# Finishing the last three output tiles of an attention kernel by column parts

## The chip, the cores and the metric

The kernel runs on one core of a Trainium2 chip. The metric is the device time of one execution in microseconds (us); the profile's span, from the first to the last instruction, is some 1.8 us shorter. Times of one kernel lie up to 1.3 us from their median (the kernel before), which matters here. So beside the time I use one stretch of each trace that does not contain the 915 us before it: from the first matmul of tile B, the first tile that the change touches, to the end of the span. Spans are given to 0.1 us, so differences of the stretch below that mean nothing.

## The reference, cut to what matters

```
xn = layernorm(x)                               # x: 2048 x 640
s  = attention(xn @ wq, k_cache, v_cache) @ wo  # 32 heads of 192, the last 512 keys
g  = silu(swiglu_ffn(xn))
return x + s * g                                # 2048 x 640, bf16
```

The output has 16 tiles of 128 rows by 640 columns. At the end of the kernel the product with `wo` for the last head pairs is still to come, and after it, tile by tile, the multiply by g and the add of a sum, `sacc`, that already holds x and the other heads' part times g.

## The kernel before: the end

```
def sc_tile():                       # two PSUM buffers of this kind, each of two halves
    return psum.tile([P, 2, 512], f32, name="sc", tag="sc")
def mm_tile():                       # and two of this kind
    return psum.tile([P, 2, 512], f32, name="mm", tag="mm")
...
def wo_mm(ps, i, qt, n, first=True, end=True):      # HD = 320 columns
    for j in range(3):
        nc.tensor.matmul(ps, OTs[i][:, 3 * qt + j, :],
            pairs[i // NB]["wo"][:, j, n * HD : (n + 1) * HD], start=..., stop=...)
...
def wo_last(b, qt, eng):
    ...
    split = b == NB - 1 and qt == 3                 # the very last tile
    sc = None if split else sc_tile()
    ps = [(mm_tile()[:, 0, :] if split else sc[:, n, :])[:, 0:HD] for n in range(2)]
    for n, cols in enumerate(halves):
        if late(i):
            wo_mm(ps[n], i - NB, qt, n, end=False)
        wo_mm(ps[n], i, qt, n, first=not late(i))
        if split:
            nc.vector.tensor_tensor(s_f[:, n, :], ps[n], g2[:, t, cols], ALU.mult)
            nc.vector.tensor_tensor(ob[:, cols], s_f[:, n, :], sacc[:, t, cols], ALU.add)
            (nc.scalar if n else nc.sync).dma_start(out=..., in_=ob[:, cols])
    if split:
        return
    nc.vector.tensor_tensor(s_f[:], sc[:, :, 0:HD], g2[:, t, :]..., ALU.mult)
    eng.tensor_tensor(ob[:], s_f[:]..., sacc[:, t, :], ALU.add)
    stores.append((t, ob))
...
for b in (2, 3):
    for qt in range(4):
        store(0 if (b, qt) == (3, 3) else 3)
        wo_last(b, qt, V if b == 3 and qt % 2 == 0 else G)   # V: VectorE, G: GpSimd
```

The last four tiles, (b, qt) = (3, 0) to (3, 3), are called A, B, C and D. Before the change A, B and C are done whole, and only D by halves. D's halves: each calls `mm_tile()` for itself, so each has a PSUM tile of its own.

The softmax here doesn't subtract the row's maximum and nothing guards it: scores larger than these inputs give would overflow.

Of the kernel before, what the change touches and what calls it, by code (L numbers as in the profile page):

```python
# [10 lines left out]
ALU = mybir.AluOpType  # L11
# [4 lines left out]
def kernel(  # L16
# [13 lines left out]
    nc = tc.nc  # L30
    P = nc.NUM_PARTITIONS

    x2 = A_x.flatten_outer_dims()
    out2 = out.flatten_outer_dims()
    Sq, D = x2.shape
# [9 lines left out]
    NB = Sq // 512  # L45
# [5 lines left out]
    HD = D // 2  # L51
    scale = float(Dh) ** -0.5
    EPS = 1e-5
    bf = dt.bfloat16
    f32 = dt.float32
# [6 lines left out]
    kk, vv, wq, wo = A_k_cache[0], A_v_cache[0], A_wq, A_wo  # L62
# [8 lines left out]
    def sc_tile():  # L71
        return psum.tile([P, 2, 512], f32, name="sc", tag="sc")

    def mm_tile():
        return psum.tile([P, 2, 512], f32, name="mm", tag="mm")
# [5 lines left out]
    g2 = res.tile([P, T, D], bf, name="g2")  # L81
# [14 lines left out]
    pairs = {}  # L96
# [68 lines left out]
    with ExitStack() as fctx:  # L165
# [154 lines left out]
        first = {f: [sc[:, s, :] for s in range(2)] for f, sc in ((0, sc_tile()), (1, sc_tile()))}  # L320
# [89 lines left out]
    finp = ctx.enter_context(tc.tile_pool(name="fin", bufs=2))  # L410
    sacc = sapool.tile([P, T, D], f32, name="sacc")

    NS = NPAIR * NB
    turn_t = smpool.tile([P, 1], f32, name="turn_t", bufs=1)
    last = NPAIR - 1
    Ps, OTs, Obs, xrs = {}, {}, {}, {}
# [89 lines left out]
    def pv_full(i, q2):  # L506

        pr, b = divmod(i, NB)
        if q2 == 0:
            Obs[i] = opool.tile([P, 4, 2, Dh], bf, name="O_b")  # L510
            tag = "OT_l" if late(i) and pr < last else "OT_b"
            OTs[i] = otpool.tile([P, 12, P], bf, name=tag, tag=tag, bufs=2 if tag == "OT_l" else 3)
        O_b, OT_b = Obs[i], OTs[i]
        alone = i < 2 or (pr == last and 2 * b + q2 < 5)
        acc = sc_tile() if alone and q2 and b < 2 else mm_tile()
        for k in range(2):
            qt = 2 * q2 + k
            for h in range(2):
                for kc in range(KC):
                    nc.tensor.matmul(  # L520
                        acc[:, k, h * 256 : h * 256 + Dh + 1],
                        Ps[i][kc][:, h, qt * P : (qt + 1) * P], V_p[:, kc, h, 0 : Dh + 1],
                        start=(kc == 0), stop=(kc == KC - 1),
                    )
        divide(i, q2, acc, alone)
# [6 lines left out]
    def late(i):  # L532
        return i // NB >= NPAIR - 2 and i % NB >= 2

    def wo_mm(ps, i, qt, n, first=True, end=True):
        for j in range(3):
            nc.tensor.matmul(  # L537
                ps, OTs[i][:, 3 * qt + j, :], pairs[i // NB]["wo"][:, j, n * HD : (n + 1) * HD],
                start=(first and j == 0), stop=(end and j == 2),
            )  # L540

# [54 lines left out]
    def wo_full(i, qt):  # L596
        pr, b = divmod(i, NB)
        t = 4 * b + qt
        sc = sc_tile()
        for n in range(2):  # L600
            wo_mm(sc[:, n, 0:HD], i, qt, n)
        s_t = sacc[:, t, :].rearrange("p (n d) -> p n d", n=2)
        if pr == 0:
            nc.vector.tensor_copy(out=s_t, in_=sc[:, :, 0:HD])
        else:
            nc.vector.tensor_tensor(s_t, s_t, sc[:, :, 0:HD], ALU.add)

        if pr == last - 1 or late(i + NB):
            nc.gpsimd.tensor_tensor(sacc[:, t, :], sacc[:, t, :], g2[:, t, :], ALU.mult)
            if pr < last - 1:  # L610
                add_x(t)
# [6 lines left out]
    def wo_last(b, qt, eng):  # L618
        i, t = last * NB + b, 4 * b + qt
        ob = xrs[t] if b < 2 else finp.tile([P, D], bf, name="ob", bufs=4)  # L620
        s_f = finp.tile([P, 2, HD], f32, name="s_f", bufs=4)
        halves = [slice(n * HD, (n + 1) * HD) for n in range(2)]
        split = b == NB - 1 and qt == 3
        sc = None if split else sc_tile()
        ps = [(mm_tile()[:, 0, :] if split else sc[:, n, :])[:, 0:HD] for n in range(2)]
        for n, cols in enumerate(halves):
            if late(i):
                wo_mm(ps[n], i - NB, qt, n, end=False)
            wo_mm(ps[n], i, qt, n, first=not late(i))
            if split:  # L630
                nc.vector.tensor_tensor(s_f[:, n, :], ps[n], g2[:, t, cols], ALU.mult)
                nc.vector.tensor_tensor(ob[:, cols], s_f[:, n, :], sacc[:, t, cols], ALU.add)
                (nc.scalar if n else nc.sync).dma_start(
                    out=out2[t * P : (t + 1) * P, cols], in_=ob[:, cols]
                )
        if split:
            return
        nc.vector.tensor_tensor(  # L638
            s_f[:], sc[:, :, 0:HD], g2[:, t, :].rearrange("p (n d) -> p n d", n=2), ALU.mult
        )  # L640
        eng.tensor_tensor(ob[:], s_f[:].rearrange("p n d -> p (n d)"), sacc[:, t, :], ALU.add)
        stores.append((t, ob))

    def store(left):
        while len(stores) > left:
            t, ob = stores.pop(0)
            nc.sync.dma_start(out=out2[t * P : (t + 1) * P, :], in_=ob[:])
# [19 lines left out]
    for pr in range(NPAIR):  # L667
        for b in range(NB):
            i = pr * NB + b
# [23 lines left out]
        for b in range(NB):  # L693
            i = pr * NB + b
# [15 lines left out]
    i = last * NB  # L710
    V, G = nc.vector, nc.gpsimd
# [3 lines left out]
    for b, q2, more in ((0, 0, (2, 1)), (0, 1, (3, 0)), (1, 0, (3, 1)), (1, 1, None)):  # L715
        for k in range(2):
            wo_last(b, 2 * q2 + k, G)
        if more:
            pv_full(i + more[0], more[1])
    for b in (2, 3):  # L720
        for qt in range(4):
            store(0 if (b, qt) == (3, 3) else 3)
            wo_last(b, qt, V if b == 3 and qt % 2 == 0 else G)


# [28 lines left out]
```

## Time and profile before

| | before |
|---|---|
| time, median of the 5 runs beside the changed kernel | 927.31 us (926.93 to 928.28) |
| span in the trace | 925.4 us |
| from tile B's first matmul (915.53) to the end | 9.87 us |
| last store issued at | 922.63 us |
| from that issue to the end of the span | 2.77 us |

In the timeline a row gives the start, the duration (of a merged group, from its first start to its last end), engine, line, what is written and read, the shape, and in brackets the idle time of the engine before the row and what ended it. In the chain of waits a row is start, length, and the work that the end depended on; "issue" is the short time between a release and the start.

### The profile page before, as it was taken

How to read it: one execution, taken by the hardware profiler on the slowest of the kernel's cores; microseconds unless marked ns; L12 is line 12 of the kernel's file. 1: busy time of each engine (PE TensorE's matmuls, PEld its weight loads, DVE VectorE, ACT ScalarE, POOL GpSimd, SP SyncE). 2: the span in 40 equal slices, each digit the busy share in tenths (PEclk: the TensorE clock that was granted, in tenths of full speed). 3: DMA queues.
4: the chain of work that ended last, by engine and by line, in shares of the span. 5: the costliest groups of instructions: out<-in, count | busy, mean ns of one | idle time of the engine just before them, and what ended most of it. 6: DMA issues, size and time to landing. Idle time of an engine off the chain costs nothing.

```text
span 925.4 us, 25770 instructions
## 1 busy us (share of the span) xinstructions
PE 917.3 (99%) x11085; PEld 624.9 (68%) x11101; DVE 575.6 (62%) x844; ACT 473.8 (51%) x847; POOL 100.1 (11%) x387
## 2 busy tenths in 40 slices
PE   9999999999999999999999999999999999999997
PEld 5455556575858585868686867676767777776665
DVE  6433331467676767676766667676767676767655
ACT  4222222556464646565555565656555555556561
POOL 0000000000000000000000000000000000002976
PEclk9999999999999999999999999999999999999999
DMA  9321510044544445444536262536362717162624
GB/s 298 72 56 33 114 35 1 1 77 89 87 79 83 83 80 86 75 90 70 95 60 106 59 107 55 111 53 113 46 119 42 124 36 129 36 129 76 135 57 140
DMA packets 243810, 77.18 MB, mean 83 GB/s; under 512 B 224624, under 2 KB 243696, under 8 KB 243696
## 3 DMA queue, kind: packets, MB, share of 16 engines
q1 hardware_dynamic: 242640, 74.72, 41.5%
q8 instruction: 87, 1.43, 0.7%
q10 hardware_dynamic: 1056, 0.82, 0.3%
q14 instruction: 27, 0.22, 0.1%
HBM read 39.45 MB, written 2.62 MB: 45 GB/s over the span
## 4 chain that ended last, share of the span: by engine, by line
PE 98%; DMA 1%; DVE 0%; issue 0%; ACT 0%; DVEq 0%
PE mm L428 22%; PE sc L563 19%; PE sc L442 18%; PE mm L468 16%; PE sc L276 11%; PE mm L298 6%; PE sc L537 3%; PE mm L520 2%; DMA wg_sb<-in_B_w_gate_dram 1%; PE mm L276 0%; PE mm L311 0%; DMA OT_b<-O_b 0%; PE sc L520 0%; DMA x_t<-in_A_x_dram 0%; DVE s_f L638 0%
## 5 line engine op out<-in xcount | busy, mean ns | idle before, releaser
L446 ACT ACTIVATE p_t<-sc 128x1024 bf16<-128x1024 f32 x254 | 253.0, 1022 | 130.5 <-PE sc L442 130.5
L433 DVE TENSOR_REDUCE qT<-mm 128x512 bf16<-128x1024 f32 x189 | 231.2, 1223 | 104.8 <-PE mm L428 102.4
L498 ACT ACTIVATE O_b<-mm,r 128x192 bf16<-128x192 f32 x486 | 164.6, 421 | 183.1 <-issue 159.9
L428 PE MATMUL mm<-xnT,wq_p 64*128 64x512 bf16 x1890 | 237.7, 377 | 0.0
L563 PE MATMUL sc<-wo_p,OT_b 64*128 64x320 bf16 x2592 | 217.4, 296 | 0.5 <-DMA OT_b<-O_b 0.5
L588 DVE TENSOR_TENSOR sacc<-sacc,sc 128x640 f32<-128x640 f32 x200 | 164.1, 821 | 78.3 <-PE sc L563 78.3
L442 PE MATMUL sc<-qT,khat 64*128 64x512 bf16 x1524 | 198.3, 377 | 0.0
L468 PE MATMUL mm<-V_p,p_t 64*128 64x193 bf16 x3520 | 186.4, 243 | 0.0
L468 PEld LDWEIGHTS <-p_t 64*128 64x128 bf16 x3584 | 162.6, 94 | 12.0
L428 PEld LDWEIGHTS <-wq_p 64*128 64x128 bf16 x1890 | 105.6, 94 | 96.0 <-issue 0.5
L563 PEld LDWEIGHTS <-OT_b 64*128 64x128 bf16 x2592 | 139.9, 94 | 22.7 <-DMA OT_b<-O_b 1.1
L442 PEld LDWEIGHTS <-khat 64*128 64x128 bf16 x1536 | 85.6, 94 | 79.2 <-issue 2.9
L551 POOL MEMSET turn_t<- 128x1 f32 x328 | 32.2, 98 | 697.9 <-PE mm L468 474.6
L284 DVE TENSOR_TENSOR hT<-sc,sg 128x512 bf16<-128x512 f32 x46 | 31.7, 690 | 85.2 <-ACT sg L283 85.1
L283 ACT ACTIVATE sg<-sc 128x512 bf16<-128x512 f32 x46 | 27.3, 596 | 72.4 <-PE sc L276 72.4
L276 PE MATMUL sc<-xnT,wg_sb 128*128 128x512 bf16 (+1 forms) x248 | 58.6, 354 | 1.0 <-DMA wg_sb<-in_B_w_gate_dram 0.4
L276 PE MATMUL sc<-xnT,wu_sb 128*128 128x512 bf16 (+1 forms) x259 | 59.1, 355 | 0.1
L298 PE MATMUL mm<-wd_sb,hT 128*128 128x320 bf16 x384 | 56.6, 300 | 0.0
L487 DVE RECIPROCAL r<-mm 128x4 f32<-128x4 f32 x124 | 22.7, 183 | 48.1 <-PE mm L468 36.3
L298 PEld LDWEIGHTS <-hT 128*128 128x128 bf16 x384 | 37.5, 98 | 18.9
L276 PEld LDWEIGHTS <-wu_sb 128*128 128x128 bf16 x285 | 26.3, 98 | 26.9
L276 PEld LDWEIGHTS <-wg_sb 128*128 128x128 bf16 x285 | 26.3, 98 | 23.5 <-DMA wg_sb<-in_B_w_gate_dram 0.5
(67 smaller groups left out, 373.1 us busy)
## 6 DMA issues: line engine op xcount, KB each, us to landing
wo_p<-in_A_wo_dram SPq DMA_DIRECT2D x16, 480.0 KB, 4.6
K_p<-in_A_k_cache_dram SPq DMA_DIRECT2D x32, 192.0 KB, 3.4
V_p<-in_A_v_cache_dram SPq DMA_DIRECT2D x32, 192.0 KB, 3.0
wq_p<-in_A_wq_dram SPq DMA_DIRECT2D x64, 80.0 KB, 3.1
wq_p<-in_A_wq_dram SPq DMA_DIRECT2D x16, 160.0 KB, 3.5
x_r<-in_A_x_dram SPq DMA_DIRECT2D x16, 160.0 KB, 3.9
x_t<-in_A_x_dram SPq DMA_DIRECT2D x14, 160.0 KB, 3.0
OT_b<-O_b SPq DMA_TRANSPOSE x124, 2.8
```

The source lines that it names most:

```text
L276: nc.tensor.matmul(out, w_sb[:, c, f * P : (f + 1) * P], xnT[:, c, qc], start=(c == 0), stop=(c == NC - 1),)
L284: nc.vector.tensor_tensor(hTs[b][:, f, :], u, sg[:], ALU.mult)
L298: nc.tensor.matmul(dn[:, 0:HD], hTs[b][:, f, ti * P : (ti + 1) * P], wd_sb[:, f, cols], start=(f == 0), stop=(f == NF - 1),)
L428: nc.tensor.matmul(q_ps[:, h, :], pairs[pr]["wq"][r, c, j * P : (j + 1) * P], xnT[r, c, b * 512 : (b + 1) * 512], start=(c == 0), stop=(c ...
L433: nc.vector.reduce_sum(qTs[i][:, j, :], q_ps[:, :, :].rearrange("p h n -> p n h"), axis=AX.X)
L442: nc.tensor.matmul(sc[:, h, :], khat[r, j, ks], qT[r, j, :], start=(j == 0), stop=(j == 2))
L446: nc.scalar.activation(p_t[:, :, :], sc[:, :, :], ACT.Exp, scale=scale)
L468: m = nc.tensor.matmul(acc[:, k, h * 256 : h * 256 + Dh + 1], Ps[i][kc][r, h, qt * P : (qt + 1) * P], V_p[r, kc, h, 0 : Dh + 1], start=(p ...
L498: nc.scalar.activation(O_b[:, qt, h, :], a_k[:, h, 0:Dh], ACT.Copy, scale=r[:, k, h, :])
L551: st["turn"] = nc.gpsimd.memset(turn_t[:], 0.0)
L563: m = nc.tensor.matmul(ps[:, n, 0:HD], OTs[i][r, 3 * qt + j, :], pairs[i // NB]["wo"][r, j, n * HD : (n + 1) * HD], start=(turn == 0 and j ...
L588: nc.vector.tensor_tensor(s_t, s_t, sc[:, :, 0:HD], ALU.add)
```

## The change

Its intent: when the last matmul is done, less work should be left on VectorE. B, C and D are cut by columns; some adds go to GpSimd; the very last part is only 128 columns wide, so that its multiply and add are short.

```
     def wo_mm(ps, i, qt, n, first=True, end=True):
+        wo_cols(ps, i, qt, slice(n * HD, (n + 1) * HD), first, end)
+    def wo_cols(ps, i, qt, cols, first=True, end=True):   # the same three matmuls, any columns
...
+    def wo_parts(qt, parts):
+        i, t = NS - 1, 4 * (NB - 1) + qt
+        ob = finp.tile([P, D], bf, name="ob", bufs=4)
+        s_f = finp.tile([P, D], f32, name="s_f", tag="s_f", bufs=4)
+        tiles, c0, d0 = [sc_tile() if qt == 2 else mm_tile()], 0, 0
+        for n, (width, eng, queue) in enumerate(parts):
+            cols, c0 = slice(c0, c0 + width), c0 + width
+            if n == 2:
+                tiles.append(sc_tile())
+            ps = tiles[n // 2][:, n % 2, 0:width]
+            wo_cols(ps, i - NB, qt, cols, end=False)
+            wo_cols(ps, i, qt, cols, first=False)
+            nc.vector.tensor_tensor(s_f[:, cols], ps, g2[:, t, cols], ALU.mult)
+            eng.tensor_tensor(ob[:, cols], s_f[:, cols], sacc[:, t, cols], ALU.add)
+            if queue:
+                queue.dma_start(out=out2[t * P : (t + 1) * P, d0:c0], in_=ob[:, d0:c0])
+                d0 = c0
...
-    for b in (2, 3):
-        for qt in range(4):
-            store(0 if (b, qt) == (3, 3) else 3)
-            wo_last(b, qt, V if b == 3 and qt % 2 == 0 else G)
+    for b, qt in ((2, 0), (2, 1), (2, 2), (2, 3), (3, 0)):
+        store(3)
+        wo_last(b, qt, V if (b, qt) == (3, 0) else G)
+    store(1)
+    wo_parts(1, ((HD, G, None), (HD, V, nc.sync)))
+    store(0)
+    wo_parts(2, ((HD, G, None), (HD, G, nc.sync)))
+    wo_parts(3, ((256, V, None), (256, G, nc.scalar), (128, V, nc.sync)))
```

The branch for `split` in `wo_last` is gone (cut here). Parts 0 and 1 of a tile lie in one PSUM tile, `tiles[0]`, in its two halves, `[:, 0, :]` and `[:, 1, :]`; the prediction calls them banks.

More of the change, by code (lines that the diff above doesn't have):

```diff
@@ L535, in wo_mm @@
     def wo_mm(ps, i, qt, n, first=True, end=True):
+        wo_cols(ps, i, qt, slice(n * HD, (n + 1) * HD), first, end)
+    def wo_cols(ps, i, qt, cols, first=True, end=True):
         for j in range(3):
             nc.tensor.matmul(
-                ps, OTs[i][:, 3 * qt + j, :], pairs[i // NB]["wo"][:, j, n * HD : (n + 1) * HD],
+                ps, OTs[i][:, 3 * qt + j, :], pairs[i // NB]["wo"][:, j, cols],
                 start=(first and j == 0), stop=(end and j == 2),
@@ L621, in wo_last @@
         s_f = finp.tile([P, 2, HD], f32, name="s_f", bufs=4)
-        halves = [slice(n * HD, (n + 1) * HD) for n in range(2)]
-        split = b == NB - 1 and qt == 3
-        sc = None if split else sc_tile()
-        ps = [(mm_tile()[:, 0, :] if split else sc[:, n, :])[:, 0:HD] for n in range(2)]
-        for n, cols in enumerate(halves):
-            if late(i):
-                wo_mm(ps[n], i - NB, qt, n, end=False)
-            wo_mm(ps[n], i, qt, n, first=not late(i))
-            if split:
-                nc.vector.tensor_tensor(s_f[:, n, :], ps[n], g2[:, t, cols], ALU.mult)
-                nc.vector.tensor_tensor(ob[:, cols], s_f[:, n, :], sacc[:, t, cols], ALU.add)
-                (nc.scalar if n else nc.sync).dma_start(
-                    out=out2[t * P : (t + 1) * P, cols], in_=ob[:, cols]
-                )
-        if split:
-            return
+        sc = sc_tile()
+        for n in range(2):
+            if late(i):
+                wo_mm(sc[:, n, 0:HD], i - NB, qt, n, end=False)
+            wo_mm(sc[:, n, 0:HD], i, qt, n, first=not late(i))
         nc.vector.tensor_tensor(
@@ L642, in wo_last @@
         stores.append((t, ob))
+    def wo_parts(qt, parts):
[13 more added lines that the diff above has]
+            if queue:
+                queue.dma_start(
+                    out=out2[t * P : (t + 1) * P, d0:c0], in_=ob[:, d0:c0]
+                )
+                d0 = c0
     def store(left):
```

## The prediction

> **What bounds the kernel now.** I read the page first: busy time, then the chain that ended last.
>
> ```profile
> PE 917.3 (99%) x11085; PEld 624.9 (68%) x11101; DVE 575.6 (62%) x844; ACT 473.8 (51%) x847; POOL 100.1 (11%) x387
> ```
>
> TensorE is busy for all but 8 us of the 925.4 us span. The change touches only the last three of the 16 final output tiles, so I went to the chain of waits and the timeline from 905 us on. There are eight tiles of the last two query blocks, each 12 matmuls of 320 columns, one tile every 1.63 us; call the last four A, B, C and D (the change cuts B, C and D). The chain of waits in order of time (start, length, what):
>
> ```profile
> 906.50 0.84 DVE s_f L638
> 907.34 0.04 issue
> 907.38 11.59 PE sc L537 x84
> 918.97 0.03 issue
> ...
> 919.06 0.83 DVE s_f L638
> ...
> 920.66 0.49 DVE s_f L631
> 921.15 0.02 issue
> 921.18 0.49 DVE ob L632
> 921.67 0.41 DVE s_f L631
> 922.08 0.02 issue
> 922.11 0.49 DVE ob L632
> ```
>
> The reader should see three things. TensorE sets the end until 918.97; then VectorE does, with about 3.5 us of multiplies and adds behind one another; then the last store and the close of the program run from 922.60 to 925.4, 2.8 us. And 907.38 shows what a semaphore from VectorE costs TensorE: a multiply that began at 906.50 let the matmul go 0.88 us later, 0.06 after its own 0.82. The timeline of VectorE and of TensorE gives the pieces:
>
> ```profile
> 915.80 0.82 DVE L638 TENSOR_TENSOR s_f<-sc,g 128x640 f32<-128x640 f32 x1 [0.81 <-PE sc L537]
> 916.66 0.83 DVE L641 TENSOR_TENSOR ob<-s_f,sacc 128x640 bf16<-128x640 f32 x1
> 917.43 0.82 DVE L638 TENSOR_TENSOR s_f<-sc,g 128x640 f32<-128x640 f32 x1
> 919.92 0.82 DVE L641 TENSOR_TENSOR ob<-s_f,sacc 128x640 bf16<-128x640 f32 x1
> 920.66 0.48 DVE L631 TENSOR_TENSOR s_f<-mm,g 128x320 f32<-128x320 f32 x1
> ```
> ```profile
> 918.79 0.57 PE L537 MATMUL mm<-wo_p,OT_l 128*128 128x320 bf16 x3
> 919.20 0.57 PE L537 MATMUL mm<-wo_p,OT_b 128*128 128x320 bf16 x3
> ```
>
> Three matmuls start every 0.407 us (919.20 minus 918.79, with rounding), 0.136 us each, so six take 0.815. Tile C's matmuls gave way to D's at 918.79 and its multiply began at 919.06: 0.27 us from the last issue to VectorE's start. A multiply costs 0.82 at 640 columns and 0.48 at 320, hence 1.06 ns per column and 0.14 fixed; I take 0.42 at 256 and 0.28 at 128 (estimates from these rows). Independent VectorE instructions follow each other slightly faster than their durations: 917.43 minus 916.66 is 0.77 for a 640-wide add, and 921.59 minus 921.18 is 0.41 for a 320-wide one. GpSimd's 640-wide adds take 1.55 (rows of the tile ob).
>
> **What the Trainium skill says.** "PSUM — Partial Sum Buffer", section "PSUM bank collisions raise a hardware error", asks for a guard between TensorE and a reader by bank and quadrant, and says that different banks may be used at once. The trace agrees: VectorE reads tile C at 919.06 while TensorE writes D at its usual pace. "TensorE: Matmul & The Clock Gate", section "Back-to-back issue gap", gives some 81 ns per matmul at 128 columns in a stream with weight loads; the trace has none of that width, but 0.084 us at 193 columns (16 in 1.34 us). "GPSIMD Engine Reference", section 3.1, gives a two-input add of 2048 columns as 4497 ns; with this trace's 1.55 us at 640, the line through both is 2.09 ns per column and 0.21 fixed, so about 0.88 us at 320 and 0.75 at 256 (estimates). "DMA: Bandwidth & Descriptors", section "Anatomy of one DMA", gives a fixed part of some 2 us; this trace's 80 KB stores land in 1.6 and the 160 KB ones in 1.8, so size hardly counts.
>
> **The change part by part.** *Intended gain.* B's add goes half to VectorE and half to GpSimd; C's 0.82 add leaves VectorE for GpSimd; D becomes parts of 256, 256 and 128 columns, the middle add on GpSimd and its store of 128 KB on the second queue. The matmuls cover the same columns (12 more instructions, the narrowest six perhaps 0.49 instead of 0.41 us on half as many columns as a 256 part's 0.65). Were nothing else changed, VectorE would run B's two multiplies from 917.43, its add at about 918.35, C's two from 918.76, D's first from about 919.72, D's second near 920.5, and GpSimd would finish D's middle add at about 921.75; the last store would go about 0.85 us earlier than 922.63, less 0.1 for its size.
>
> *Added wait.* The built program of the changed kernel says otherwise. I read the count that each matmul waits for. Before, the eight tiles wait only for what used their buffer earlier, and D's halves lie in two tiles so that neither waits for the other. After, the two parts of B, of C, and the first two of D are halves of one PSUM tile, and the second part's first matmul waits for VectorE at 838, 841 and 843. Counting VectorE's instructions back from the last (847), those are exactly the multiplies of the *first part of the same tile*. The parts lie in different banks, so the chip needs no such wait, but the program has it: TensorE must stop after each first part until VectorE has read it. The third part of D has its own tile and waits for nothing recent.
>
> *Sum.* B's first part is issued from 915.53 to 916.35 as now. VectorE is then in A's multiply and A's add, so B's first multiply starts at 917.43; TensorE goes on at 917.43+0.48+0.06=917.97. **Stall: 1.62 us.** B's second part ends at 918.79, multiply at 919.06, its add at 919.58, so VectorE is free at 919.99. C's first part is issued by 919.60, its multiply would be possible at 919.87 but starts at 919.99; TensorE goes on at 920.53. **Stall: 0.93.** C's second part ends at 921.34, multiply at 921.61. D's first 256 columns end at 922.00 (0.655 for six), multiply from 922.27 to 922.68, TensorE goes on at 922.74. **Stall: 0.74.** D's second part ends at 923.40, multiply 923.67 to 924.09, GpSimd's add from 924.17 (0.08 later, as at 918.33 after 918.25) to 924.92. D's third part is through TensorE at about 923.88, VectorE ends its add near 924.7. So the last store goes at about 924.95, from the second queue, against 922.63 before: 2.32 us later, plus 0.1 for 128 KB instead of 80. The stalls sum to 3.29 us; 0.85 of it comes back as the intended gain and the rest is rounding and order. **Predicted: 927.31 + 2.4 = 929.7 us**, span about 927.8.
>
> **Rivals.** *The waits are harmless.* If the wait were met before TensorE arrives, the result is the intended gain, about 0.75 us: 926.6. For it: an independent reading of the code would expect this, as the parts are in different banks. Against it: the counts name multiplies that cannot start before their own part is done, so each stall is at least 0.27+0.42+0.06. *VectorE or GpSimd sets the end anyway.* GpSimd's middle add ends within 0.3 us of VectorE's last; if it takes 0.62 (in proportion to 1.55) the end is 0.13 earlier, and VectorE's own last add then bounds it. That is worth at most 0.2 us either way: 929.5 to 929.9. *TensorE's clock drops in the stalls.* In the window from 921 us to the end, where TensorE has nothing to do, the granted clock averages 0.84; up to 921 it is 1.00. The stalls are 1.6 us at most, shorter than the 4.4 us of that window, so I hold this for unlikely; a half clock in C and D would add about 2 us: 931.7. *The stores are hidden or collide.* The earlier stores of A and B are no longer near the end in either case; 16 output stores of 160 KB land in 1.8 to 3.1 us, and only D's count.
>
> **Range and chances.** The mechanism is read from the built program, and its terms from rows; I give it 85 in 100, the intended gain alone 10, anything larger 5. The runs before scatter by 0.7 us about the middle, and the other terms by some 0.4. That gives 927.6 to 931.0 for eight in ten. Every version lies within 0.5% of 927.31, far from 2%: faster 0.005, same 0.985, slower 0.01.
>
> **What would show it.** Three idle gaps on TensorE ended by VectorE's multiplies, near 916.4 (1.6 us), 919.6 (0.9) and 922.0 (0.7), would prove the wait; no such gaps, the first rival. VectorE's and GpSimd's adds of 256 columns would show 0.43 and 0.75. The chain of waits should alternate between TensorE and VectorE from B on and end in GpSimd's add and the 128 KB store. The prediction is wrong if the gaps are missing, if the stalls are there but hidden behind something that I hold for short, or if an idle TensorE comes back at a lower clock.

## The result, and the profile after

The changed kernel takes 929.61 us (median of 5 runs, 929.16 to 929.84), the kernel before 927.31 in the same rounds: 2.30 us slower. The ratio is 1.0024, 95% interval 1.001 to 1.0037, so the slowing is clear of noise although far inside 2%. Ratios and their intervals here are from the runs of both kernels in the same rounds; they can differ by 0.0001 or 0.0002 from the ratio of the medians or of the means.

The page's busy times of the changed kernel hardly move; the end of a 927 us kernel can't be seen in them:

```profile
PE 917.9 (99%) x11107; PEld 623.9 (67%) x11107; DVE 575.9 (62%) x847; ACT 473.8 (51%) x847; POOL 101.9 (11%) x390
```

The chain of waits of the changed kernel from tile B on, in which VectorE and TensorE now take turns:

```profile
916.13 0.03 DVE ob L633
916.16 0.71 issue
916.87 0.49 DVE s_f L649
917.36 0.04 issue
917.40 0.99 PE mm L540 x6
...
919.35 0.49 DVE s_f L649
919.85 0.04 issue
919.89 0.97 PE sc L540 x6
...
921.63 0.43 DVE s_f L649
922.06 0.04 issue
922.10 0.83 PE mm L540 x6
```

Three times a multiply (`s_f`) on VectorE releases a group of matmuls 0.04 us after its end. Before, one release of this kind stood in the chain, at 907.38, and from there the matmuls ran through to the last tile. The timeline of TensorE's weight loads, which start and stop with the matmul stream and have no modelled ends, gives the length of the gaps in the brackets:

```profile
917.41 0.23 PEld L540 LDWEIGHTS <-OT_l 128*128 128x128 bf16 x2 [1.63 <-issue]
919.89 0.23 PEld L540 LDWEIGHTS <-OT_l 128*128 128x128 bf16 x2 [0.89 <-issue]
922.10 0.20 PEld L540 LDWEIGHTS <-OT_l 128*128 128x128 bf16 x2 [0.76 <-issue]
```

The gaps sum to 3.28 us; they lie in the middle of B, of C, and between D's first two parts. (The rows of the matmuls themselves show 1.43, 0.69 and 0.58, because the last matmul's end is drawn some 0.2 us after that of the last weight load.) Now the end of the changed kernel on VectorE, GpSimd and the two queues:

```profile
923.30 0.28 DVE L649 TENSOR_TENSOR s_f<-sc,g 128x128 f32<-128x128 f32 x1
923.51 0.72 POOL L650 TENSOR_TENSOR ob<-s_f,sacc 128x256 bf16<-128x256 f32 x1 [1.18 <-issue]
923.62 0.77 DVE L650 TENSOR_TENSOR ob<-s_f,sacc 128x128 bf16<-128x128 f32 x1
924.26 0.40 ACTq L652 DMA_DIRECT2D out_dram<-ob  x1
```

The last add is the narrow one, 128 columns, and yet it took 0.77 us, longer than the 0.49 of the 320-wide add that ended the kernel before. It ends 0.15 us after GpSimd's add beside it. The last store follows at 924.41. From B's first matmul (915.00) to the end of the span (927.4) it is 12.40 us, against 9.87: 2.53 us more, in agreement with the 2.30 in the median time, given the scatter.

### The profile page after: what moved, and what is told of

Same layout as the page of the kernel before. It is cut to its first block, busy times and chain, and to the rows that moved or that the text cites. A ratio compares the mean times of both kernels' runs of the same rounds, so it can differ in the third digit from the quotient of the medians.

```text
span 927.4 us, 25805 instructions
## 1 busy us (share of the span) xinstructions
PE 917.9 (99%) x11107; PEld 623.9 (67%) x11107; DVE 575.9 (62%) x847; ACT 473.8 (51%) x847; POOL 101.9 (11%) x390
## 3 DMA queue, kind: packets, MB, share of 16 engines
q8 instruction: 87, 1.43, 0.7%
## 4 chain that ended last, share of the span: by engine, by line
PE 98%; DMA 1%; DVE 1%; issue 0%; ACT 0%; DVEq 0%
PE mm L428 22%; PE sc L566 19%; PE sc L442 18%; PE mm L468 16%; PE sc L276 11%; PE mm L298 6%; PE sc L540 3%; PE mm L520 2%; DMA wg_sb<-in_B_w_gate_dram 1%; PE mm L276 0%; PE mm L311 0%; PE sc L520 0%; DMA OT_b<-O_b 0%; DMA x_t<-in_A_x_dram 0%; DVE s_f L649 0%; PE mm L540 0%
```

## The experiments

My theory: all of the loss comes from the second part of a shared PSUM tile waiting for VectorE's read of the first part. The rivals: that the parts cost by themselves (more instructions, more adds on GpSimd); that a gap is a fixed cost of splitting; that something other than the tiles, such as the narrow part, matters. For each run I give the time against the kernel before in the same rounds, and the stretch from B's first matmul to the end.

| run | time, us (before beside it) | ratio, 95% interval | stretch, us |
|---|---|---|---|
| before | 927.31 | | 9.87 |
| changed | 929.61 (927.31) | 1.0024, 1.001 to 1.0037 | 12.40 |
| own_tiles | 926.37 (927.02) | 0.9993, 0.998 to 1.0005 | 9.58 |
| own_again | 926.81 (927.36) | 0.9993, 0.998 to 1.0007 | 9.52 |
| before_shared | 927.44 (927.02) | 1.0003, 0.999 to 1.0015 | 10.45 |
| after_a_pool | 929.04 (927.02) | 1.0021, 1.0008 to 1.0035 | 11.87 |
| after_late_reads | 927.68 (927.02) | 1.0004, 0.9992 to 1.0017 | 10.44 |
| own_halves | 927.26 (927.36) | 0.9998, 0.9986 to 1.0011 | 9.47 |
| own_a_pool | 927.29 (927.36) | 0.9998, 0.9985 to 1.0011 | 9.99 |
| after_mid_dve | 929.37 (927.36) | 1.0021, 1.0007 to 1.0035 | 12.03 |

All outputs are right.

**own_tiles: each part in a PSUM tile of its own.** This takes away what makes the matmul wait. Parts, adds and stores stay; which of the four buffers a part gets changes with it, but no wait from that shows in the trace.

```
-        tiles, c0, d0 = [sc_tile() if qt == 2 else mm_tile()], 0, 0
+        c0, d0 = 0, 0
...
-            if n == 2:
-                tiles.append(sc_tile())
-            ps = tiles[n // 2][:, n % 2, 0:width]
+            ps = (sc_tile() if qt == 2 or n == 2 else mm_tile())[:, 0, 0:width]
```

> The changed kernel with each column part in a PSUM tile of its own; nothing else differs. Theory (the second part of a shared tile waits for the multiply of the first part): the three idle gaps of TensorE (1.63, 0.89, 0.76 us in the changed kernel) vanish, the last store goes some 0.7 to 0.9 us earlier than before the change, the time falls from 929.6 to 926.4 to 926.9 us. Rival (the parts cost by themselves: more instructions, adds on GpSimd): the time stays at 929 or more.

All three gaps are gone, and the 2.30 us with them: 926.37 us, at the lower edge of the expectation. The timeline of its matmuls through C's end and D:

```profile
917.88 0.57 PE L540 MATMUL sc<-wo_p,OT_b 128*128 128x320 bf16 x3
918.28 0.49 PE L540 MATMUL mm<-wo_p,OT_l 128*128 128x256 bf16 x3
918.61 0.49 PE L540 MATMUL mm<-wo_p,OT_b 128*128 128x256 bf16 x3
918.94 0.49 PE L540 MATMUL mm<-wo_p,OT_l 128*128 128x256 bf16 x3
919.26 0.49 PE L540 MATMUL mm<-wo_p,OT_b 128*128 128x256 bf16 x3
919.59 0.33 PE L540 MATMUL sc<-wo_p,OT_l 128*128 128x128 bf16 x3
919.76 0.33 PE L540 MATMUL sc<-wo_p,OT_b 128*128 128x128 bf16 x3
```

The groups of three follow each other without an idle bracket, across every boundary between parts. The same parts, the same adds on GpSimd and the same instruction counts on VectorE are in it, so the parts do not cost by themselves. But the stretch is only 0.29 us shorter than before the change, where I had worked out 0.75, and the last store goes 0.35 us earlier (6.75 us after B's first matmul, before 7.10), not the 0.7 to 0.9 expected; that the time still came out as expected lies within its scatter. Its timeline on VectorE and GpSimd shows why:

```profile
917.81 0.85 DVE L648 TENSOR_TENSOR ob<-s_f,sacc 128x320 bf16<-128x320 f32 x1
...
917.46 0.86 POOL L648 TENSOR_TENSOR ob<-s_f,sacc 128x320 bf16<-128x320 f32 x1 [1.27 <-DVE s_f L647]
919.14 2.59 POOL L648 TENSOR_TENSOR ob<-s_f,sacc 128x320 bf16<-128x320 f32 x3 [0.83 <-DVE s_f L647]
921.77 0.37 ACTq L650 DMA_DIRECT2D out_dram<-ob  x1
```

VectorE's add of B took 0.85 instead of 0.49 us; it ends 0.35 after GpSimd's add beside it. And GpSimd works without a pause from 919.14 to 921.73 on C's two adds and then D's middle one, so the middle add, which holds back the last store, queues. GpSimd is held in its turn: the second of these adds took 1.05 us, not 0.86, beside an add on VectorE that had started 0.13 us before it. My sum had C's adds on GpSimd out of the way.

**own_again: the same program once more**, with the next three runs.

> The same program as the run with tiles of their own, a second time on another chip perhaps, to place its small gain. From the start of tile B's matmuls to the end of the span it took 9.58 us against 9.87 before the change; theory: 9.5 to 9.7 again, and 0.2 to 0.7 us below the time before. Rival: the gain was scatter of the earlier 915 us, and the ratio to the kernel before comes out at or above 1.

926.81 against 927.36, stretch 9.52. Both times the median is lower by 0.55 to 0.65 us, and both times the interval of the ratio includes 1. This is the only version here whose median lies below both kernels by more than 0.1 us; a gain of 0.07% is likely but not proved.

**before_shared: the one wait alone, added to the kernel before.**

```
-        sc = None if split else sc_tile()
-        ps = [(mm_tile()[:, 0, :] if split else sc[:, n, :])[:, 0:HD] for n in range(2)]
+        sc = mm_tile() if split else sc_tile()
+        ps = [sc[:, n, 0:HD] for n in range(2)]
```

> The kernel before with one edit: the two halves of the very last tile are put into one PSUM tile instead of two. Theory: one gap of about 1.6 us on TensorE (it waits until 920.66+0.48+0.06 for the first half's multiply, which itself waits behind the add of the tile before), the last multiply moves from 921.59 to about 922.29, the time rises by 0.7 us to 928.0. Rival: sharing a tile costs nothing, 927.3.

The weight loads show the expected gap, in the middle of D:

```profile
921.02 0.23 PEld L537 LDWEIGHTS <-OT_l 128*128 128x128 bf16 x2 [1.63 <-issue]
```

From D's first matmul to the end it takes 7.19 us (918.61 to 925.8), against 6.61 before (918.79 to 925.4): 0.58 more. The median rose by 0.42, less than the 0.7 expected and by itself not separable from noise. The gap is shown, its price is 0.4 to 0.6 us. A gap of 1.63 us costs so little here because VectorE was 0.9 us behind anyway: before, D's second half was ready at about 920.7 (0.27 after the issue of its matmuls ended, 920.42) and its multiply started only at 921.59.

**after_a_pool: tile A's add moved from VectorE to GpSimd** in the changed kernel, so that VectorE is free when B's first part is ready.

```
-        wo_last(b, qt, V if (b, qt) == (3, 0) else G)
+        wo_last(b, qt, G)
```

> The changed kernel with the add of the tile before the three parts moved from VectorE to GpSimd, so that VectorE is free when the first part's matmuls end. Theory: the first gap shrinks from 1.63 to about 0.8 us, and the time falls by 0.4 to 0.8 us (less than the full 0.8 if the adds on the two engines get in each other's way) to 928.8 to 929.2. Rival (a gap is a fixed cost of a split tile, whatever VectorE does): the first gap stays near 1.6 us and so does the time.

```profile
917.76 0.57 PE L540 MATMUL mm<-wo_p,OT_l 128*128 128x320 bf16 x3 [0.65 <-DVE s_f L649]
920.47 0.57 PE L540 MATMUL sc<-wo_p,OT_l 128*128 128x320 bf16 x3 [0.92 <-DVE s_f L649]
```

By the weight loads, as above, these two gaps are 0.85 instead of 1.63 and 1.12 instead of 0.89; the third stays at 0.76. The second grew because VectorE's add of B, beside one on GpSimd, took 0.72 us instead of 0.49 and put off C's first multiply. The gaps sum to 0.55 less, and the stretch falls by 0.53 to 11.87. The time of 929.04 lies in the range given, but its ratio to the kernel before, 1.0021, cannot be told from the 1.0024 of the changed kernel; the trace carries this result. So the length of a gap is the time until VectorE has *finished the read*, with all that VectorE has queued before it, and not a fixed price of a split.

**after_late_reads: shared tiles kept, the multiply of part 0 emitted after the matmuls of part 1.** In the program's order the read now stands behind both writes.

```
             wo_cols(ps, i - NB, qt, cols, end=False)
             wo_cols(ps, i, qt, cols, first=False)
-            nc.vector.tensor_tensor(s_f[:, cols], ps, g2[:, t, cols], ALU.mult)
-            (the add and the store)
+            todo.append((ps, cols, c0, eng, queue))
+            for ps, cols, c1, eng, queue in todo if n else ():
+                nc.vector.tensor_tensor(s_f[:, cols], ps, g2[:, t, cols], ALU.mult)
+                (the add and the store, as before)
+            if n:
+                todo = []
```

> The changed kernel with the shared tiles kept, but the multiply of the first part emitted after the matmuls of the second part. In the built program the matmuls then wait for nothing in their own tile, and the first multiply waits for both parts. Theory: no gaps on TensorE, but the last tile's first multiply starts some 0.65 us later than with tiles of their own; 926.9 to 927.6 us. Rival: 929 or more.

No gap is left. The list of who waited for whom in the last 20 us has no line in which TensorE waits for these multiplies; the only wait of TensorE on VectorE is the one at the start of the last eight tiles that all the kernels have:

```profile
PE sc L540 <- DVE s_f L630: 0.2, 1, 0.2
```

927.68 us is 1.9 us below the changed kernel and 0.7 above the kernel before; it lies 0.08 above the range that I had given. The stretch is 0.86 us longer than with tiles of their own (10.44 and 9.58). In the built program the first multiply of each tile now waits for the last matmul of *both* parts. In the trace D shows it:

```profile
919.80 0.43 DVE L651 TENSOR_TENSOR s_f<-mm,g 128x256 f32<-128x256 f32 x1 [0.37 <-PE mm L540]
```

This is 4.84 us after B's first matmul, against 4.36 in own_tiles (919.38); the adds after it were then held beside GpSimd (256 columns took 0.82 us, 128 columns 0.77). So the dependence goes by tile in both directions: a write waits for an earlier read, and a read waits for an earlier write, anywhere in the tile.

**own_halves: with own tiles, D in two halves again.** It undoes the 128-wide last part, and with it D's add on GpSimd.

```
-    wo_parts(3, ((256, V, None), (256, G, nc.scalar), (128, V, nc.sync)))
+    wo_parts(3, ((HD, V, nc.sync), (HD, V, nc.scalar)))
```

> As with tiles of their own, but the very last tile in two halves of 320 columns, both added by VectorE, as before the change; undoes the 256, 256, 128 cut alone. Theory: the narrow last part saves nothing as it stands, because GpSimd still has tile C's second add until about 920.9 us and the middle part's add queues behind it; the stretch from tile B's first matmul to the end stays within 0.3 us of 9.58 (I work out 9.3). Rival: the narrow last part is what saves time, and the stretch grows by 0.4 us or more.

The stretch is 9.47 us, not longer than with three parts (9.58 and 9.52). The times of this run scatter from 926.29 to 928.5, so its median says little. By the trace, the narrow last part saves nothing as it stands.

**own_a_pool: with own tiles, A's add on GpSimd.** Same edit as in after_a_pool.

> As with tiles of their own, and tile A's add (0.82 us) moved from VectorE to GpSimd. VectorE, which works from 916.9 to 921.2 us without a pause, then gets its 0.82 us before that stretch. Theory: the end is bounded by the adds and multiplies on VectorE and GpSimd, GpSimd ends tile C's second add some 0.5 us earlier, and the stretch falls from 9.58 to about 9.2 us. Rival: GpSimd, 1.54 us for this add, becomes the bound and the stretch grows.

The rival came true: the stretch grew by 0.4 to 9.99 us. A's add occupied GpSimd, so B's first add began there at about 918.2, 2.7 us after B's first matmul instead of 2.4, GpSimd worked without a pause to C's end, and VectorE's adds waited beside it:

```profile
920.16 1.06 DVE L648 TENSOR_TENSOR ob<-s_f,sacc 128x256 bf16<-128x256 f32 x1
```

256 columns took 1.06 us, against 0.43 for the same add undisturbed (next run). Work moved to an engine with idle time is not free if the two engines hold each other up.

**after_mid_dve: the changed kernel with D's middle add on VectorE**, so that GpSimd does nothing beside the last add.

```
-    wo_parts(3, ((256, V, None), (256, G, nc.scalar), (128, V, nc.sync)))
+    wo_parts(3, ((256, V, None), (256, V, nc.scalar), (128, V, nc.sync)))
```

> The changed kernel with only the last tile's middle add moved from GpSimd to VectorE, so that nothing runs on GpSimd beside VectorE's last add. In the changed kernel that last add of 128 columns took 0.77 us, where 0.29 was expected. Theory (VectorE waits for GpSimd's running add, both reading two operands from SBUF): the last add takes 0.28 to 0.30 us. Rival (a narrow add is slow for another reason): 0.7 or more. The gaps stay, the last store goes at about the same time, 929.3 to 929.8 us.

```profile
924.09 0.43 DVE L650 TENSOR_TENSOR ob<-s_f,sacc 128x256 bf16<-128x256 f32 x1
924.75 0.29 DVE L650 TENSOR_TENSOR ob<-s_f,sacc 128x128 bf16<-128x128 f32 x1
```

The last add takes 0.29 us when GpSimd is idle, where it took 0.77. The Trainium skill has this in "SBUF — State Buffer", section "Who interferes with whom": a VectorE instruction with two SBUF inputs contends with a GpSimd instruction that reads SBUF, one with at most one such input, outside the two-port modes, does not. The traces agree on both counts: the adds read `s_f` and `sacc` from SBUF and were held, while the multiplies read one operand from PSUM and kept their duration beside a running GpSimd add (before the change 0.82 us at 919.06, with a GpSimd add running from 918.33). The three gaps and the time, 929.37 us, stay as expected. The stretch is 0.37 us shorter than in the changed kernel, although the last store goes as late, 9.40 us after B's first matmul against 9.41: this 32 KB store landed in 1.5 us instead of 1.8. It is issued 0.52 us after the 128 KB store here, and 0.15 after it in the changed kernel; that the two stores held each other up there is inferred from this.

## Why the prediction was right

929.7 us was predicted and 929.61 measured. Point by point:

- *The added wait.* Right, and shown by experiments: taking the shared tiles away removes the gaps and the loss, reading late removes the gaps too, and sharing one tile in the kernel before makes such a gap.
- *The three stalls.* 1.62, 0.93 and 0.74 us were worked out, 1.63, 0.89 and 0.76 measured on the weight loads (by the starts of the matmuls, which is what was worked out, 1.59, 0.86 and 0.74). That the first is so long because VectorE is still in A's multiply and add is shown by after_a_pool, where it halves.
- *The intended gain.* Mis-sized. The prediction put it at 0.85 us less 0.1; with own tiles the stretch shortens by 0.29 to 0.35. The step that failed is "GpSimd would finish D's middle add at about 921.75": counted from B's start that is 6.2 us, and in own_tiles it took 6.7 (915.02 to 921.73), for two reasons. VectorE came to D's middle multiply 0.2 us later than worked out (5.19 us after B's start, not 4.97), its add of B having been held. And GpSimd took up the middle add some 0.3 us after it could have, because C's second add, itself stretched, was in its queue ahead of it. The sum did not have that the adds on the two engines hold each other up.
- *The sum.* The number was worked out along the stalled chain itself, to a last store 9.42 us after B's first matmul; 9.41 was measured. The mis-sized gain does not enter it. The sentence that 0.85 of the 3.29 us of stalls comes back is bookkeeping beside it, and wrong in both terms. From own_tiles to the changed kernel the stretch grew by 2.82 us: TensorE's last group of three started 3.18 us later (7.92 us after B's first matmul against 4.74), 0.52 less was left from its issue to the last store (1.32 against 1.84), and the close took 0.16 longer. Less the 0.29 that own_tiles gains, this is the 2.53 in the trace. That the median then came within 0.1 us of the number is luck, as the runs scatter by more.
- *Which instruction ends it.* Wrong, and here luck helped by some 0.2 us. GpSimd's middle add ended 9.23 us after B's first matmul, with 9.39 worked out; VectorE's narrow add, worked out to end some 0.2 us before it at 9.17, ended at 9.39, since it was held for 0.48 us. So the last store went at the predicted moment, but from the other engine.
- *The costs taken from the skill.* GpSimd's adds took 0.86 us at 320 columns and 0.72 at 256 where VectorE did not hold them; 0.88 and 0.75 were estimated. The narrowest six matmuls took 0.34 us, not 0.49.
- *The other rivals.* The clock did not drop in the stalls. A window of the changed kernel (stretch, its length, busy time of the engines, granted clock, DMA):

```profile
915.50:919.00 3.50, 2.07 (x16) 1.36 (x15) 2.37 (x5) 0.00 (x0) 1.51 (x2) 1.00 0.29 98
```

The third number from the right is the clock, 1.00 here and in the windows from 919 to 921 and from 921 to 923 us, while TensorE, the first busy time, was busy only 2.07 of 3.50 us. The stores: the prediction set aside that they collide and held that size hardly counts. Size counted little (the 128 KB store landed in 1.8 us, the 80 KB ones before in 1.6), but the 32 KB store issued 0.15 us after the 128 KB one took 1.8 us too, and 1.5 where the two lay further apart (own_tiles, after_mid_dve). So a collision of 0.3 us is likely in the changed kernel; the time hides it. (There are 15 stores of 160 KB and two of 80 before the change, not 16.)

What stays open: whether own_tiles is really faster than the kernel before (two ratios of 0.9993, both intervals including 1); whether the chip would need a wait between the two halves of one PSUM tile (no run let TensorE write one while VectorE read the other); and whether a division of the adds that keeps the two engines apart would bring the rest of the intended gain.

## What to carry to other kernels

When a tile is cut into parts so that reading one overlaps with computing the next, give each part its own buffer: here the dependence went by the whole PSUM tile, not by the half in use, and turned an overlap into a pause of up to 1.63 us. Look in the built program at which count each first matmul of a part waits for; it names the culprit before anything runs. Before moving an add to an idle engine, check what runs beside it: two adds that both read SBUF on VectorE and GpSimd went one after the other.

## What the Trainium skill lacked or had wrong

- **No page has it:** a wait in the built program can be wider than the guard that a page asks for. "PSUM — Partial Sum Buffer" asks for a guard by bank and quadrant; here the two halves of one tile, which I take for two banks, waited for each other, for 1.63, 0.89 and 0.76 us, and with separate tiles for 0.
- **"TensorE: Matmul & The Clock Gate", section "Back-to-back issue gap":** some 81 ns per matmul at 128 columns in a stream with weight loads, and 131 at 512. Here three 128-column matmuls, each with its weight load, started in 0.17 us (919.59 to 919.76 in own_tiles), 57 ns each, and 320 columns already took 136. Six such matmuls are no sustained stream; but both numbers fit the formula N / 2.4 + 2.5 ns (56 and 136) that the section keeps for isolated matmuls.
- **"SBUF — State Buffer", section "Who interferes with whom":** right that such adds contend, but without a size for this pair. Here VectorE was held until GpSimd's add ended: the 128-column add took 0.77 us instead of 0.29 and ended 0.15 after it, the 320-column one 0.85 instead of 0.49 and ended 0.35 after it. Where VectorE's add had started first, GpSimd's took 1.05 us instead of 0.86.
